# Chunk-selected attention with a gated output stage, rewritten around a list scheduler, shared PSUM banks, quadrant convolution and half-precision bounds

## The chip, the cores and the metric

The kernel runs on one core of one Trainium2 chip. The metric is the device time of one execution in microseconds (us), from the device's own record. The kernel before takes 294.87 us, the median of 3 runs (294.83 to 296.1).

## The reference

Inputs are q, k and v of shape (4 batches, 8 heads, 768 positions, 64 dimensions) in fp32 and three weight arrays. What is computed, cut to what matters:

```python
# attention over the 6 best chunks of 32 keys, per query row
k_chunks = k.reshape(B, H, 24, 32, D)
k_min, k_max = np.min(k_chunks, axis=3), np.max(k_chunks, axis=3)
ub = np.sum(np.maximum(q[..., None, :] * k_min[:, :, None], q[..., None, :] * k_max[:, :, None]), axis=-1)
ub = np.where(causal_chunk, ub, -1e9)
top_chunks = np.argsort(ub, axis=-1)[..., -6:]
scores = (q @ k.T) / 8                       # masked to the chosen chunks and to keys at or before the row
attn = softmax(scores)
x = (attn @ v), heads side by side           # (4, 768, 512)

# gated stage
gate_pre[t, c] = sum over 5 taps i of conv_w[i, c] * x[t - 4 + i, c]   # causal, one filter per channel
out = (sigmoid(gate_pre) * (x @ w_val)) @ w_out                         # w_val, w_out: 512 x 512
```

An upper bound per query and chunk chooses six chunks; attention sees only keys in them; the result goes through a short causal convolution per channel that gates a linear map, and through a second linear map. The output is fp32.

## The kernel before

Two heads make a pair; there are 16 pairs, four to a batch. A pair goes through three lists of steps, and a fourth list holds the gated stage.

- `kq_steps` loads nothing itself (the loads are issued two pairs ahead by `load_kq` and `load_v` on SyncE's queue). It transposes K and Q on TensorE in fp32 with an identity (L155, L178), three 128x128 blocks to a PSUM bank, so each of K and Q takes two halves of 384 columns. ScalarE copies K out, scaled by 1/8, to fp16 (`KE`, L159), and VectorE reduces the same bank to the maximum and minimum of each chunk (L163, L164). `kblock` forms the per-chunk bounds relative to the first chunk (L167 to L172) in fp32 (`KB`). Q is copied to fp32 (`q32`, L181); GpSimd casts it to fp16 (`QU`, L183); VectorE makes max(q, 0) (`rq`, L185). GpSimd casts V to fp16 with a column of ones (`VA`, L190).
- `sel_steps` computes the bounds with fp32 matmuls, max(q,0) times (max - min) plus q times min (L207, L209), for five of the six tiles of 128 rows; the first tile needs no choice. VectorE adds the causal fill (L211), takes the top eight of each row (L219), compares with the sixth (L224) and has TensorE transpose the 0/1 result (L233). The copy of that (L236) goes into spare partitions of `QU`: opposite them in `KE` lie rows with -30 over one chunk each, so the score matmul itself subtracts 30 from the keys of chunks not chosen.
- `attn_steps` computes scores with keys on the partitions and queries on the columns, in banks of 512 columns (L271, L291), takes the exponential on ScalarE into fp16 (L275, L295), zeroes the triangle above the diagonal on GpSimd (L264, L280), multiplies by V with the column of ones for the denominator (L304), divides on VectorE (L306, L307), and transposes the result to channels by positions, `xT` (L314, L316). No maximum is subtracted ahead of the exponential.
- The gated stage works per batch on 128 channels at a time. The convolution is a matmul with diagonal matrices, five taps times a high and a low fp16 part of the weight, so ten matmuls of 384 columns per half (L334). The forty diagonals are built by GpSimd (L379) from `cwT` and `cwl`. ScalarE takes tanh (L339); `moe_val` multiplies by w_val (L348) and VectorE gates it (L352); `moe_out` multiplies by w_out (L359), and ScalarE's copy (L362) is stored (L363).

The order is set by hand. At iteration i the attention of pair i, the selection of pair i+1, the K and Q work of pair i+2 and the gated steps due at i are merged by their relative place in each list:

```python
merge(attn_steps(i), sel_steps(i + 1), kq_steps(i + 2), moe[i])
```

PSUM has three tags: "w" (three banks, every transposition, bound, convolution, value and output), "s" (three banks, scores) and "av" (two banks).

Of the kernel before, what the change touches and what calls it, by code (L numbers as in the profile page):

```python
# [13 lines left out]
AX = mybir.AxisListType  # L14


@with_exitstack
def kernel(
# [10 lines left out]
    nc = tc.nc  # L29
# [8 lines left out]
    PEN = -30.0  # L38
    NPAIR = (B * H) // 2
    HB = S // 2  # L40


    HP = (slice(0, 64), slice(64, 128))
    CP = (slice(64, 64 + NCH), slice(0, NCH))
    KP = (slice(0, 64 + NCH), slice(0, 128))

    CC = (1, 0)
    SELT = NT - 1

    ident_np = np.eye(128, dtype=np.float32)  # L50
    identh_np = np.eye(128, dtype=np.float16)
    e_np = np.zeros((64, S), dtype=np.float16)
    for c in range(NCH):
        e_np[c, c * CH:(c + 1) * CH] = PEN
    cfill_np = np.zeros((128, SELT, 2, NCH), dtype=np.float32)
    for it in range(1, NT):
        for p in range(128):
            cfill_np[p, it - 1, :, (it * 128 + p) // CH + 1:] = -1.0e9
    cfill_np = cfill_np.reshape(128, SELT * 2 * NCH)

    ident_dr = nc.inline_tensor(ident_np, name="identc")
    identh_dr = nc.inline_tensor(identh_np, name="identh")
    e_dr = nc.inline_tensor(e_np, name="echunk")
    cfill_dr = nc.inline_tensor(cfill_np, name="cfill")

    cpool = ctx.enter_context(tc.tile_pool(name="cpool", bufs=1))
    npool = ctx.enter_context(tc.tile_pool(name="npool", bufs=3))
    hpool = ctx.enter_context(tc.tile_pool(name="hpool", bufs=2))
    ppool = ctx.enter_context(tc.tile_pool(name="ppool", bufs=2))
    mpool = ctx.enter_context(tc.tile_pool(name="mpool", bufs=2))  # L70
    ps = ctx.enter_context(tc.tile_pool(name="ps", bufs=3, space=bass.MemoryType.PSUM))

    ident = cpool.tile([128, 128], FP, tag="ident")
    identh = cpool.tile([128, 128], F16, tag="identh")
    cfill = cpool.tile([128, SELT * 2 * NCH], FP, tag="cfill")
    wval_sb = cpool.tile([128, NCT, DM], F16, tag="wval")
    wout_sb = cpool.tile([128, NCT, DM], F16, tag="wout")
    w32 = cpool.tile([128, 2, NCT, DM], FP, tag="w32")
    cwn = cpool.tile([KSZ * NCT, 128], FP, tag="cwn")
    cwT = cpool.tile([128, KSZ * NCT], FP, tag="cwT")  # L80
    cwh = cpool.tile([128, KSZ * NCT], F16, tag="cwh")
    cwl = cpool.tile([128, KSZ * NCT], FP, tag="cwl")
    diag = cpool.tile([128, KSZ * NCT, 2, 128], F16, tag="diag")
    xT = cpool.tile([128, 2 * NCT, S + 4], F16, tag="xT")
    KE = [cpool.tile([128, 2, S], F16, tag=f"KE{i}", name=f"KE{i}") for i in range(3)]
    QU = [cpool.tile([128, 2, S], F16, tag=f"QU{i}", name=f"QU{i}") for i in range(3)]
    VA = [cpool.tile([128, 2, NT, D + 1], F16, tag=f"VA{i}", name=f"VA{i}") for i in range(3)]
    KB = [cpool.tile([128, 2, 2 * NCH], FP, tag=f"KB{i}", name=f"KB{i}") for i in range(2)]
    NS = [cpool.tile([128, SELT, 128], F16, tag=f"NS{i}", name=f"NS{i}") for i in range(2)]

    def bank(shape, dt=FP, tag="w", bufs=3):
        return ps.tile(shape, dt, tag=tag, name=f"ps_{tag}", bufs=bufs)

    nat = {}

    def load_kq(p):
        b, h0 = p // NCT, 2 * (p % NCT)
        kn = npool.tile([128, NT, 128], FP, tag="kn", name="kn")
        qn = npool.tile([128, NT, 128], FP, tag="qn", name="qn")
        vn = npool.tile([128, NT, 128], FP, tag="vn", name="vn")  # L100
        nat[p] = (kn, qn, vn)
        for t, src in ((kn, k), (qn, q)):
            for hh in range(2):
                nc.sync.dma_start(out=t[:, :, hh * 64:(hh + 1) * 64],
                                  in_=src[b, h0 + hh].rearrange("(t p) d -> p t d", p=128))

    def load_v(p):
        b, h0 = p // NCT, 2 * (p % NCT)
        for hh in range(2):
            nc.sync.dma_start(out=nat[p][2][:, :, hh * 64:(hh + 1) * 64],  # L110
                              in_=v[b, h0 + hh].rearrange("(t p) d -> p t d", p=128))


    nc.sync.dma_start(out=ident, in_=ident_dr.ap())
    load_kq(0)
    for i in range(3):
        for hh in range(2):
            nc.sync.dma_start(out=KE[i][HP[1 - hh], hh, :], in_=e_dr.ap())
    nc.sync.dma_start(out=cfill, in_=cfill_dr.ap())
    nc.sync.dma_start(out=identh, in_=identh_dr.ap())  # L120
    load_v(0)
    load_kq(1)
    load_v(1)
    nc.sync.dma_start(out=cwn, in_=moe_conv_w.rearrange("k (c p) -> (k c) p", p=128))
    nc.sync.dma_start(out=w32[:, 0], in_=moe_w_val.rearrange("(ct c) e -> c ct e", c=128))
    nc.sync.dma_start(out=w32[:, 1], in_=moe_w_out.rearrange("(et e) o -> e et o", e=128))

    for i in range(2):
        nc.gpsimd.memset(KB[i], 0.0)
    for i in range(3):  # L130
        nc.vector.memset(QU[i][HP[1], 0, :], 0.0)
        nc.vector.memset(QU[i][HP[0], 1, :], 0.0)
    for i in range(2):
        nc.gpsimd.memset(NS[i], 0.0)
    for i in range(3):
        nc.gpsimd.memset(VA[i][:, :, :, D:D + 1], 1.0)
    nc.vector.memset(xT[:, :, 0:4], 0.0)

    st = {}


    def kq_steps(p):
        kn, qn, vn = nat.pop(p)
        ke, qu, va, kb = KE[p % 3], QU[p % 3], VA[p % 3], KB[p % 2]
        kmx = hpool.tile([128, NCH], FP, tag="kmx", name="kmx")
        kmn = hpool.tile([128, NCH], FP, tag="kmn", name="kmn")
        kmd = hpool.tile([128, NCH], FP, tag="kmd", name="kmd")
        q32 = hpool.tile([128, S], FP, tag="q32", name="q32")
        rq = hpool.tile([128, S], FP, tag="rq", name="rq")
        st[p] = dict(ke=ke, qu=qu, va=va, kb=kb, q32=q32, rq=rq)  # L150

        def khalf(w):
            pt = bank([128, HB])
            for tl in range(3):
                nc.tensor.transpose(out=pt[:, tl * 128:(tl + 1) * 128],  # L155
                                    in_=kn[:, 3 * w + tl, :], identity=ident)
            sl = slice(w * HB, (w + 1) * HB)
            for hh in range(2):
                nc.scalar.activation(out=ke[HP[hh], hh, sl], in_=pt[HP[hh]],  # L159
                                     func=AF.Copy, scale=0.125)  # L160
            cs = slice(w * 12, (w + 1) * 12)
            ptc = pt.rearrange("p (c t) -> p c t", t=CH)
            nc.vector.tensor_reduce(out=kmx[:, cs], in_=ptc, axis=AX.X, op=ALU.max)  # L163
            nc.vector.tensor_reduce(out=kmn[:, cs], in_=ptc, axis=AX.X, op=ALU.min)  # L164

        def kblock():
            nc.vector.tensor_tensor(out=kmd, in0=kmx, in1=kmn, op=ALU.subtract)  # L167
            for hh in range(2):
                hp, c0 = HP[hh], CC[hh] * NCH
                nc.vector.tensor_scalar(out=kb[hp, 0, c0:c0 + NCH], in0=kmd[hp],  # L170
                                        scalar1=kmd[hp, 0:1], scalar2=None, op0=ALU.subtract)
                nc.vector.tensor_scalar(out=kb[hp, 1, c0:c0 + NCH], in0=kmn[hp],  # L172
                                        scalar1=kmn[hp, 0:1], scalar2=None, op0=ALU.subtract)

        def qhalf(w):
            pt = bank([128, HB])
            for tl in range(3):
                nc.tensor.transpose(out=pt[:, tl * 128:(tl + 1) * 128],  # L178
                                    in_=qn[:, 3 * w + tl, :], identity=ident)
            sl = slice(w * HB, (w + 1) * HB)  # L180
            nc.scalar.activation(out=q32[:, sl], in_=pt, func=AF.Copy)  # L181
            for hh in range(2):
                nc.gpsimd.tensor_copy(out=qu[HP[hh], hh, sl], in_=q32[HP[hh], sl])  # L183
            a = max(w * HB, 128)
            nc.vector.tensor_scalar(out=rq[:, a:(w + 1) * HB], in0=q32[:, a:(w + 1) * HB],  # L185
                                    scalar1=0.0, scalar2=None, op0=ALU.max)

        def vcast():
            for hh in range(2):
                nc.gpsimd.tensor_copy(out=va[:, hh, :, 0:D],  # L190
                                      in_=vn[:, :, hh * 64:(hh + 1) * 64])

        return [lambda: khalf(0), lambda: khalf(1), lambda: qhalf(0), kblock, lambda: qhalf(1),
                vcast]
# [254 lines left out]
```

## Time and profile before

| quantity | value |
|---|---|
| median of 3 runs | 294.87 us |
| profiled execution, first to last instruction (span) | 292.5 us |
| runs' median less that span | 2.4 us |
| TensorE matmuls busy | 241.3 us, 82% of the span |
| TensorE weight loads busy (they overlap matmuls) | 171.6 us |
| VectorE, ScalarE, GpSimd busy | 155.2, 160.2, 121.8 us |
| mean granted TensorE clock | 0.959 of full |
| first score matmul in the chain of waits | at 27.07 us |
| DMA moved | 28.46 MB, mean 97 GB/s |

Only the span of the profiled execution is on record, not a separate device time, so the 2.4 us between it and the median of the runs stands for what lies around the span. Busy times of TensorE count every matmul with its passage through the pipeline, and consecutive matmuls overlap; how often a new one starts is read from the chain of waits or from the timeline.

### The profile page before, as it was taken

How to read it: one execution, taken by the hardware profiler on the slowest of the kernel's cores; microseconds unless marked ns; L12 is line 12 of the kernel's file. 1: busy time of each engine (PE TensorE's matmuls, PEld its weight loads, DVE VectorE, ACT ScalarE, POOL GpSimd, SP SyncE). 2: the span in 40 equal slices, each digit the busy share in tenths (PEclk: the TensorE clock that was granted, in tenths of full speed). 3: DMA queues.
4: the chain of work that ended last, by engine and by line, in shares of the span. 5: the costliest groups of instructions: out<-in, count | busy, mean ns of one | idle time of the engine just before them, and what ended most of it. 6: DMA issues, size and time to landing. Idle time of an engine off the chain costs nothing.

```text
span 292.5 us, 5928 instructions
## 1 busy us (share of the span) xinstructions
PE 241.3 (82%) x2161; PEld 171.6 (59%) x2161; DVE 155.2 (53%) x522; ACT 160.2 (55%) x329; POOL 121.8 (42%) x261
## 2 busy tenths in 40 slices
PE   2383926509998897999998999999989999999994
PEld 1181614405757575776666667676757676765551
DVE  3547162404676674858573657666645667631160
ACT  3232713503768659465674774756747765467313
POOL 2416189999254436243433253425251624223000
PEclk9999975956999999999999999999999999999999
DMA  7999992205162554242456343332211000003105
GB/s 165 211 304 245 218 175 54 54 0 110 33 132 55 110 110 99 66 108 56 107 151 159 91 114 86 70 87 61 74 74 38 36 2 0 2 2 143 73 2 215
DMA packets 80746, 28.46 MB, mean 97 GB/s; under 512 B 75962, under 2 KB 76622, under 8 KB 80718
## 3 DMA queue, kind: packets, MB, share of 16 engines
q1 hardware_dynamic: 80718, 28.09, 40.9%
q8 instruction: 17, 0.28, 0.4%
q14 instruction: 11, 0.09, 0.1%
HBM read 21.79 MB, written 6.29 MB: 96 GB/s over the span
## 4 chain that ended last, share of the span: by engine, by line
PE 66%; POOL 12%; ACT 10%; issue 3%; SPq 3%; DVE 2%; DMA 2%; ACTq 0%; POOLq 0%
PE ps_w L334 17%; PE ps_s L271 10%; POOL diag L379 7%; PE ps_av L304 6%; PE ps_w L348 6%; PE ps_w L359 6%; PE ps_w L209 6%; ACT P L275 5%; PE ps_w L207 5%; PE ps_w L155 4%; PE ps_w L178 2%; POOL QU L183 2%; PE ps_w L314 2%; ACT KE L159 2%; ACT osb L362 1%
## 5 line engine op out<-in xcount | busy, mean ns | idle before, releaser
L275 ACT ACTIVATE P<-ps_s 128x512 f16<-128x512 f32 x160 | 87.8, 606 | 57.1 <-PE ps_s L271 56.8
L271 PE MATMUL ps_s<-QU,KE 88*128 88x512 f16 (+5 forms) x224 | 54.9, 336 | 7.1 <-ACT P L275 4.1
L264 POOL TENSOR_SCALAR_AFFINE_SELECT P<-P 128x256 f16<-128x256 f16 (+1 forms) x80 | 29.0, 364 | 71.1 <-ACT P L275 58.3
L334 PE MATMUL ps_w<-xT,diag 128*128 128x384 f16 x320 | 57.8, 331 | 0.0
L304 PE MATMUL ps_av<-VA,P 128*128 128x65 f16 x672 | 33.4, 196 | 21.9 <-POOL P L264 19.9
L304 PEld LDWEIGHTS <-P 128*128 128x128 f16 x672 | 28.4, 99 | 32.0 <-POOL P L264 26.2
L159 ACT ACTIVATE KE<-ps_w 64x384 f16<-64x384 f32 x64 | 31.0, 485 | 26.9 <-PE ps_w L155 26.5
L183 POOL CAST QU<-q 64x384 f16<-64x384 f32 x64 | 35.1, 548 | 24.6 <-ACT q L181 22.7
L334 PEld LDWEIGHTS <-diag 128*128 128x128 f16 x320 | 31.0, 99 | 21.4 <-issue 1.9
L339 ACT ACTIVATE g<-ps_w 128x384 f32<-128x384 f32 x32 | 15.9, 498 | 30.5 <-PE ps_w L334 30.5
L209 PE MATMUL ps_w<-KB,q 128*128 128x48 f32 x160 | 32.3, 285 | 0.0
L163 DVE TENSOR_REDUCE kmx<-ps_w 128x12 f32<-128x384 f32 x32 | 17.8, 555 | 26.7 <-ACT KE L159 26.6
L236 DVE COPY QU<-ps_w 24x640 f16<-24x640 f16 x32 | 15.5, 484 | 29.9 <-PE ps_w L233 29.4
L207 PE MATMUL ps_w<-KB,rq 128*128 128x48 f32 x160 | 31.2, 278 | 0.0
L271 PEld LDWEIGHTS <-KE 88*128 88x128 f16 (+1 forms) x224 | 21.1, 101 | 16.8 <-issue 10.8
L280 POOL TENSOR_SCALAR_AFFINE_SELECT P<-P 128x256 f16<-128x256 f16 x32 | 13.1, 408 | 31.4 <-ACT P L275 31.3
L207 PEld LDWEIGHTS ps_w<-KB,rq 128*128 128x128 f32 x160 | 25.9, 202 | 0.3
L155 PE MATMUL ps_w<-ident,kn 128*128 128x128 f32 x96 | 17.7, 300 | 9.7 <-DMA kn<-in_k_dram 9.7
L209 PEld LDWEIGHTS ps_w<-KB,q 128*128 128x128 f32 x160 | 25.7, 202 | 0.0
L348 PE MATMUL ps_w<-xT,wval_sb 128*128 128x384 f16 x128 | 23.9, 325 | 1.8 <-ACT q L181 1.8
L190 POOL CAST VA<-vn 128x384 f16<-128x384 f32 x32 | 16.5, 516 | 20.4 <-PE ps_av L304 12.9
L359 PE MATMUL ps_w<-wout_sb,gv 128*128 128x512 f16 x96 | 23.8, 379 | 0.7 <-ACT osb L362 0.7
(46 smaller groups left out, 309.0 us busy)
## 6 DMA issues: line engine op xcount, KB each, us to landing
kn<-in_k_dram SPq DMA_DIRECT2D x32, 192.0 KB, 3.3
qn<-in_q_dram SPq DMA_DIRECT2D x32, 192.0 KB, 3.4
vn<-in_v_dram SPq DMA_DIRECT2D x32, 192.0 KB, 3.3
out_dram<-osb SPq DMA_DIRECT2D x24, 256.0 KB, 2.0
w<-in_moe_w_val_dram SPq DMA_DIRECT2D x1, 1024.0 KB, 5.6
w<-in_moe_w_out_dram SPq DMA_DIRECT2D x1, 1024.0 KB, 7.9
KE<-echunk SPq DMA_DIRECT2D x6, 96.0 KB, 2.7
cfill<-cfill SPq DMA_DIRECT2D x1, 120.0 KB, 2.3
```

The lines of the kernel that those rows point to most:

```text
L155: nc.tensor.transpose(out=pt[:, tl * 128:(tl + 1) * 128], in_=kn[:, 3 * w + tl, :], identity=ident)
L159: nc.scalar.activation(out=ke[HP[hh], hh, sl], in_=pt[HP[hh]], func=AF.Copy, scale=0.125)
L183: nc.gpsimd.tensor_copy(out=qu[HP[hh], hh, sl], in_=q32[HP[hh], sl])
L207: nc.tensor.matmul(out=pu[:, it - 1, :], lhsT=rq[:, ts], rhs=kb[:, 0, :], start=True, stop=False)
L209: nc.tensor.matmul(out=pu[:, it - 1, :], lhsT=q32[:, ts], rhs=kb[:, 1, :], start=False, stop=True)
L264: nc.gpsimd.affine_select(out=ap, in_=ap, pattern=[[0, n], [1, 128]], compare_op=ALU.is_ge, fill=0.0, base=0, channel_multiplier=-1)
L271: nc.tensor.matmul(out=pq[:, col:col + n], lhsT=ke[KP[hh], hh, jt * 128:(jt + 1) * 128], rhs=qu[KP[hh], hh, q0:q0 + n], start=True, stop=True)
L275: nc.scalar.activation(out=pt, in_=pq, func=AF.Exp)
L304: nc.tensor.matmul(out=pav[:, qt, :], lhsT=where[hh, jt, qt], rhs=va[:, hh, jt, :], start=(jt == 0), stop=(jt == qt))
L334: nc.tensor.matmul(out=pg, lhsT=diag[:, ki * NCT + ct, part, :], rhs=xT[:, slot, w * HB + ki:w * HB + ki + HB], start=(n == 0), stop=(n == ...
L348: nc.tensor.matmul(out=pv, lhsT=wval_sb[:, ct, et * 128:(et + 1) * 128], rhs=xT[:, slot0 + ct, 4 + w * HB:4 + (w + 1) * HB], start=(ct == ...
L359: nc.tensor.matmul(out=po, lhsT=gv[b, et][:, s * 128:(s + 1) * 128], rhs=wout_sb[:, et, :], start=(et == 0), stop=(et == NCT - 1))
```

## The change

The kernel is written again with the same stages. The parts:

1. **Order.** Every step is a `Node` with an engine, a guessed duration, its reads and writes and a priority. `Plan.schedule` is a list scheduler that places the nodes on the engines' queues and issues the program in the order of the starts it finds. Offsets of each kind of step from its pair's base (`OFF`, in ns, with `PERIOD` between pairs) are constants.
2. **PSUM.** One tile holds all eight banks. A step asks for one bank or an aligned two, and the scheduler hands them out. So K and Q are transposed into two banks and copied in one instruction of 768 columns, both heads' scores go into two banks and one exponential of 1024 columns, and both heads' AV results are divided in one instruction.
3. **Bounds.** q is split into fp16 high and low parts (`QH`, `QL`), max(q,0) likewise (`RH`, `RL`), and the chunk bounds likewise (`KB`). Six fp16 matmuls of 48 columns per tile replace the two fp32 ones; the first tile takes two. `KB` is no longer relative to the first chunk, and only the four chunks on the diagonal get the causal fill.
4. **Softmax guard.** The largest bound of a row becomes a 33rd row beside the 24 mask rows (copied by `m`), opposite a row of -0.125, and the exponential adds 10: the exponent is score - bound/8 + 10.
5. **Convolution.** Once per batch and two 128-channel slots, all work is in 64x64 diagonals. For each tap and part, four matmuls go to the four quarters of the array: rows 0-63 or 64-127 of a slot (`r`) and slot `c` of the two. The 64x64 diagonals are built by two VectorE multiplies instead of forty GpSimd ones. The columns of w_val and rows of w_out are loaded in the matching channel order.
6. **Engines.** K is scaled to fp16 by GpSimd from an SBUF copy, K's reductions read that copy, Q's casts are VectorE's, one half of the mask copy is ScalarE's. Constants (identities, mask rows, fill) are made on the chip by GpSimd and no longer loaded. Loads go into four buffers; output has four buffers, and the last batch's evictions alternate between ScalarE and VectorE. Eight matmuls on zeros open TensorE's queue.

The core of the diff (a line of dots marks what is left out):

```diff
-    merge(kq_steps(0))
-    merge(sel_steps(0), kq_steps(1))
-    for i in range(NPAIR):
...
+    def schedule(self):
...
+                t0 = min(c[0] for c in cand)
+                t, n, pick = min((c for c in cand if c[0] <= t0 + self.slack),
+                                 key=lambda c: (c[1].prio, c[1].i))
...
+    order = plan.schedule()
+    with tc.manual_schedule():
+        for n in order:
+            n.fn()

-    ps = ctx.enter_context(tc.tile_pool(name="ps", bufs=3, space=bass.MemoryType.PSUM))
+    psum = pp.tile([128, 8, 512], FP, tag="psum", name="psum")

-                nc.tensor.matmul(out=pu[:, it - 1, :], lhsT=rq[:, ts], rhs=kb[:, 0, :],
-                                 start=True, stop=False)
-                nc.tensor.matmul(out=pu[:, it - 1, :], lhsT=q32[:, ts], rhs=kb[:, 1, :],
-                                 start=False, stop=True)
+            for it in range(1, NT):
+                n = 0
+                for lhs, part, kind in ((QH, 0, 1), (RH, 0, 0), (QH, 1, 1), (RH, 1, 0), (QL, 0, 1), (RL, 0, 0)):
+                    term(it, lhs, kbs(part, kind), n == 0, n == 5)
+                    n += 1

+        add(f"K32{p}", ACT, t_act(S), 124, base + OFF["KT"], lambda: nc.scalar.activation(
+            out=K32[w].rearrange("p (a n) -> p a n", a=2), in_=b3(kbk)[:, :, 0:HB], func=AF.Copy),
+            [("kps", p)], [("K32", w)], [kbk])
+                lambda h=h: nc.gpsimd.tensor_scalar(out=KE[t3][HP[h], h, :], in0=K32[w][HP[h]],
+                                                    scalar1=0.125, scalar2=None, op0=ALU.mult),
+            lambda: nc.vector.tensor_copy(out=QH[w], in_=Q32[w]), [("Q32", w)], [("QH", w)])
+            lambda: nc.vector.tensor_scalar(out=RH[w], in0=QH[w], scalar1=0.0, scalar2=None, op0=ALU.max),
+                lambda h=h: nc.vector.tensor_copy(out=QU[t3][HP[h], h, :], in_=QH[w][HP[h]]),
+            lambda: nc.gpsimd.tensor_tensor(out=QL[w][:, 128:S], in0=Q32[w][:, 128:S],
+                                            in1=QH[w][:, 128:S], op=ALU.subtract),
+            lambda: nc.vector.scalar_tensor_tensor(out=RL[w][:, 128:S], in0=QH[w][:, 128:S], scalar=0.0,
+                                                   in1=QL[w][:, 128:S], op0=ALU.is_gt, op1=ALU.mult),

-            nc.scalar.activation(out=pt, in_=pq, func=AF.Exp)
+                out=pt[:, :, 0:n], in_=psum[:, bk.at:bk.at + 2, 0:n], func=AF.Exp, bias=bias),

-            for ki in range(KSZ):
-                for part in range(2):
-                    nc.tensor.matmul(out=pg, lhsT=diag[:, ki * NCT + ct, part, :],
-                                     rhs=xT[:, slot, w * HB + ki:w * HB + ki + HB],
-                                     start=(n == 0), stop=(n == 2 * KSZ - 1))
+                    for n in range(2 * KSZ):
+                        ki, part = n // 2, n % 2
+                        for r in range(2):
+                            rp = HP[r]
+                            for c in range(2):
+                                nc.tensor.matmul(out=psum[HP[c], gb.at + r, 0:HB],
+                                                 lhsT=diag[rp, part, ki * NCT + 2 * j + c, :],
+                                                 rhs=xT[rp, s0 + 2 * j + c, hw * HB + ki:hw * HB + ki + HB],
+                                                 start=(n == 0), stop=(n == 2 * KSZ - 1))

-                nc.gpsimd.tensor_scalar(out=diag[:, i, part, :], in0=identh,
-                                        scalar1=w[:, i:i + 1], scalar2=None, op0=ALU.mult)
+                nc.vector.tensor_tensor(
+                    out=diag[:, part], in0=i64.unsqueeze(1).to_broadcast([128, n, 64]),
+                    in1=src.unsqueeze(2).to_broadcast([128, n, 64]), op=ALU.mult)
+            eng = DVE if last and s % 2 else ACT
```

## The prediction

> **What bounds the kernel now.** I read the page first: TensorE (PE) is busy 82% of 292.5 us, no other engine over 55%. Stretch by stretch (busy us of each engine, granted clock, DMA share, GB/s) this is not one regime:
>
> ```profile
> 20.00:50.00 30.00, 15.67 (x113) 10.64 (x112) 14.56 (x51) 10.84 (x24) 18.60 (x33) 0.83 0.99 188
> 50.00:100.00 50.00, 37.59 (x360) 27.30 (x359) 24.85 (x88) 26.91 (x57) 34.22 (x68) 0.86 0.34 74
> 150.00:200.00 50.00, 47.14 (x452) 33.85 (x451) 31.90 (x113) 33.19 (x70) 21.04 (x47) 1.00 0.43 107
> ```
>
> The columns after the length are PE, weight loads, VectorE (DVE), ScalarE (ACT), GpSimd (POOL). From 100 us on PE is the bound, with 47 of 50 us; before that POOL is busier than later, PE is half idle and its clock is down to 0.83 of full. The chain of waits (start, length, engine, what, count) says why, and gives the steady period:
>
> ```profile
> 24.43 1.97 DVE rq L185
> ...
> 38.73 6.37 POOL diag L379 x10
> ...
> 137.00 0.41 PE ps_av L304 x13
> ...
> 138.69 3.26 PE ps_w L334 x20
> ...
> 144.98 0.86 PE ps_w L359 x4
> ...
> 192.20 1.31 PE ps_w L348 x8
> ...
> 198.63 3.26 PE ps_w L334 x20
> ...
> 285.97 0.61 ACT osb L362
> 286.59 2.02 DMA out_dram<-osb
> ```
>
> Building the forty diagonals (L379, 24.9 us of POOL) holds the early pairs. Then the convolution of every fourth pair stands 59.94 us apart (138.69 to 198.63), so a pair costs 14.98 us.
>
> **What a pair costs PE.** A group's mean ns counts the pipeline's depth; what queues is the step from one start to the next, and the chain shows it: convolution 3.26/20 = 0.163 us for 384 columns, value 1.31/8 = 0.163, output 0.86/4 = 0.216 for 512 (so 0.00042 per column), attention times V 0.41/13 = 0.032. The timeline shows the two fp32 kinds:
>
> ```profile
> 206.00 0.39 PE L207 MATMUL ps_w<-KB,rq 128*128 128x48 f32 x2
> 206.22 0.39 PE L209 MATMUL ps_w<-KB,q 128*128 128x48 f32 x2
> ...
> 207.78 0.51 PE L155 MATMUL ps_w<-ident,kn 128*128 128x128 f32 x3
> 208.13 0.38 PE L271 MATMUL ps_s<-QU,KE 88*128 88x512 f16 x1
> ```
>
> Two fp32 bound records per 0.22, so 20 per pair are 2.20; three fp32 transposes take 0.35 or less (0.11 each). A pair now: transposes 12 x 0.11 = 1.3, bounds 2.2, mask transposes 5 x 0.055 = 0.3, scores 5376 columns = 2.26, AV 42 x 0.032 = 1.34, back transposes 0.33, convolution 20 x 0.163 = 3.26, value 1.3, output 6 x 0.216 = 1.3. Sum 13.6; the other 1.4 of the 14.98 is PE waiting. Over 16 pairs PE has 217 us of work, so 75 of the span are start, waits and tail.
>
> **The change, part by part.**
> *Bounds in fp16.* Twenty fp32 records go (2.20). Thirty-two fp16 matmuls of 48 columns come, each like an AV matmul (65 columns, own weights, 0.032): 1.02. Gain 1.18 per pair.
> *Convolution in quadrants.* Per batch four groups of ten steps, each step four 64x64 matmuls of 384 columns in four different quarters of the array. No row shows quarters. If the four run beside each other a step is one stream, 0.163, and a group 1.63; if they queue, four streams, 0.652 and 6.52. Issue doesn't forbid the first: AV shows a load and a matmul every 0.032, so forty pairs issue in 1.28. I take 1.63, the row of the same 384 columns, because each of the four uses its own partitions in, its own partitions or bank out, and nothing in the order stands between them. Per pair (a group per pair) 1.63 instead of 3.26.
> The Trainium skill, "TensorEngine Tiling (Array Packing)", Tiling Modes, says that tiles load and multiply in parallel, which agrees with 1.63. The same page speaks against it under Restrictions: column tiling switches off the fast weight load; "TensorE: Matmul & The Clock Gate", LDWEIGHTS, prices a load at columns/1.2 ns, so four loads of 64 would be about 0.213 per step, and as an estimate the total would grow by 8 us. No row here shows it.
> *The rest of PE.* A sixth mask transpose (0.33 for six), and weights with 97 rows instead of 88, free (88 and 128 rows both stream 512 columns in the same step). A pair after: 1.3 + 1.02 + 0.33 + 2.26 + 1.34 + 0.33 + 1.63 + 1.3 + 1.3 = 10.8; sixteen, 173 us.
> *ACT.* L275 starts every 0.48 for 512 columns, L295 0.27 for 256: 0.06 + 0.00083 per column. After, per pair: K and Q copies and one mask half, each 768 wide (3 x 0.69), five exponentials of 1024 and one of 256 (5 x 0.90 + 0.27), tanh 0.69, 1.5 outputs (0.72): 8.25. The guard is a bias and one more weight row, so nothing here. Covered by 10.8.
> *DVE.* L163 repeats every 0.47 for 384, so about 1.04 ns per column plus 0.06. Per pair: two reductions of 768 (1.72), normalising (0.87), gating (0.87), two PSUM copies of 768 at L316's rate (0.95), eleven top-8 steps (0.82), comparison, fill, reciprocal (0.54), key bounds (0.55), QH (0.46), RH and two QU copies (0.26 each, if narrow copies run at twice the fp32 rate; 0.46 each if not), RL 0.73: about 8.3 to 8.9.
> *POOL.* The diagonals' 24.9 go to DVE as two multiplies of 1280 columns (2.8). L264 takes 0.41 for 256 and 0.29 for 128; casts 0.51 for 384 and 1.9 to 2.07 for 2048. Per pair: four triangles (2.1), V cast (0.85), two KE scalings of 768 (0.85 each as casts; L379's 0.60 for 128 columns is the high end, 3.6), QL with two inputs (between a cast, 0.74, and 3.0 at L379's rate; I double the cast, 1.5), guard copy 0.15: 6.3. The low values are nearer, being plain streams like the casts; at the high ends POOL would hold 13.3 per pair, 16 x 13.3 + 24 of start, tail and surroundings = 237.
> *A price hidden in that.* The row that speaks against it, from the timelines of POOL and DVE:
>
> ```profile
> 24.12 2.07 POOL L366 CAST wval_sb<-w 128x2048 f16<-128x2048 f32 x1
> ...
> 24.36 2.04 DVE L185 TENSOR_SCALAR rq<-q 128x384 f32<-128x384 f32 x1
> ```
>
> An SBUF-to-SBUF DVE step that takes 0.36 at 215.00 in the same timeline lasted 2.04 here, as long as POOL's cast beside it ran. The new DVE work has five such steps per pair (QH, RH, QU twice, RL) and some small ones. The mean of the 16 wide L185 rows is 0.590, so 0.23 over 0.36; nine such waits are 2.1, DVE 10.4 to 11.0 per pair. That is beside a pair of 12.2 (below), so I charge nothing, with up to 12.2 - 11 of cover left.
> The Trainium skill, "SBUF — State Buffer", section on two separate sides, states this as an exclusive lock for a whole instruction; by that rule each of the nine can lose a full POOL instruction, and the estimate would be that of the whole of rival 3.
> *Start.* First scores stand at 27.07 now. After: the keys are the first load; POOL builds constants until about 8.3 (0.8 in, 0.8 of identities, 5.7 of mask rows: a memset like L134's 0.63 for 640, four selects of 768 at 0.87, two memsets; 1.0 of fills), scales KE to 10.0, makes QL to 11.5, DVE makes RL to 12.2, bounds, top-8 and comparison to 14.3, transposes and copies to 15.3; eight hand-overs of 0.16 to 0.2 (a matmul lasts 0.33 while the next starts at 0.163): 17. By then PE has done 4.0 of its 173.
> *Waits and tail.* The list order and the shared banks move everything, and no row prices that. Ends: no waits at all, or twice now's. I keep the 1.4 per pair, since the stages and their lengths are the same: 23. After PE's last matmul 6.6 pass now (285.9 to 292.5); with a fourth output buffer the last eviction no longer waits: 4.5.
> *Sum.* 17 + 169 + 23 + 4.5 = 213.5 of span. The median of the runs, 294.87, is 2.4 over the profiled span of 292.5, so 216.
>
> **The rivals.**
> 1. Forecast: quarters beside each other, PE still the bound. 216, by itself 204 (waits halved) to 228 (waits half as long again). Chance 0.62.
> 2. Quarters overlap only in twos, or their loads queue: a step is 0.326 or something between. Up to 16 x 1.63 = 26 more: 225 to 242. For: no row shows four at once. Against: 0.032 per load and matmul. 0.16.
> 3. The order doesn't hold: DVE loses a whole POOL instruction (6.3 / 9 = 0.7 on average) at each of nine steps, so DVE is 8.3 + 6.3 = 14.6 per pair and the bound. 16 x 14.6 + 17 + 4.5 + 2.4 = 258, halfway 237. For: 24.36. Against: most L185 rows wait far less. 0.12.
> 4. The other side: the convolution doesn't do what it says; quarters queue and their loads are not covered, each matmul costing its stream and a load of 0.099 (the mean of LDWEIGHTS on L334), 0.262. 640 x 0.262 = 168 instead of 26: 358. It decides from 0.164 per quarter matmul on: there 640 x 0.164 = 105 instead of 26 eats the whole gain of 79. With covered loads, 0.163, it comes to 294, no change: 0.04. Slower: 0.06.
>
> **How the numbers follow.** Faster is rivals 1 to 3, 0.90; same 0.04; slower 0.06. About 0.5% is what a measurement of this kernel can tell from no change. The range takes the forecast's own ends and reaches through rival 2 and the halfway case of 3: 204 to 245.
>
> **What would show it.** Convolution steps of about 0.163 for four records (right), 0.33 or 0.65 (rivals 2, 4); the bound matmuls 0.032 apart; first scores near 17 us; no POOL diagonals; a pair's period near 12.2 with PE over 85% busy between 60 and 190 us and full clock. Wrong: PE idle ended mostly by DVE or POOL, DVE steps on SBUF data several times their shortest, KE scalings of 3 us.

## The result, and the profile after

The changed kernel takes 261.4 us (median of 4 runs, 259.9 to 262.8) beside 294.9 before: a ratio of 0.886, with a 95% interval of 0.881 to 0.891. The direction was right; the size was not. 216 was forecast, 261.4 lies outside 204 to 245, and the gain is 33 us where 79 were expected.

The stretches of the changed kernel (length, then busy us of PE, weight loads, DVE, ACT and POOL, granted clock, DMA share, GB/s):

```profile
0.00:20.00 20.00, 7.72 (x33) 4.31 (x33) 15.34 (x25) 3.72 (x4) 17.36 (x28) 0.74 1.01 228
20.00:50.00 30.00, 22.40 (x254) 17.18 (x255) 25.48 (x79) 16.84 (x19) 21.15 (x20) 0.72 0.86 208
50.00:100.00 50.00, 36.86 (x572) 26.47 (x572) 41.17 (x122) 33.71 (x40) 41.10 (x46) 0.97 0.51 113
100.00:150.00 50.00, 40.85 (x552) 29.14 (x549) 46.98 (x122) 34.13 (x43) 33.96 (x32) 0.97 0.41 101
150.00:200.00 50.00, 41.29 (x632) 28.85 (x633) 39.36 (x106) 31.62 (x39) 33.09 (x34) 0.97 0.15 44
200.00:250.00 50.00, 46.09 (x641) 29.72 (x640) 20.06 (x52) 28.91 (x37) 13.19 (x20) 1.00 0.13 49
```

Before, PE was busy 47 of 50 us from 100 us on. Now it is busy 37 to 41 through the middle and gets back to 46 only after 200 us, when the last keys have been prepared. From 50 to 100 us DVE and POOL are the fullest engines, at 41 each; then DVE alone, at 47; from 150 to 200 no engine is over 42. The steps wait for one another across engines, as the chain of waits shows further down. The costliest groups show what lies on POOL (busy us, mean ns of one, then the idle time before it):

```profile
L440 POOL TENSOR_SCALAR KE<-K 64x768 f16<-64x768 f32 x32 | 72.3, 2258 | 23.1 <-PE psum L577 19.2
L598 POOL TENSOR_SCALAR_AFFINE_SELECT P<-P 128x512 f16<-128x512 f16 (+1 forms) x64 | 36.1, 580 | 27.0 <-ACT P L584 26.2
L655 PE MATMUL psum<-xT,diag 64*64 64x384 f16 x640 | 28.7, 329 | 2.2 <-DVE xT L634 2.2
L459 POOL TENSOR_TENSOR QL<-Q,QH 128x640 f16<-128x640 f32 x16 | 22.9, 1432 | 9.8 <-DVE QH L450 8.5
```

One scaling of K to KE takes 2.26 us on average, 2.12 at its shortest, where the forecast took 0.85. The chain of waits goes over three engines in nearly equal parts, and by line it names KE first; between 121 and 129 us (start, length) four POOL steps stand in it one behind the other:

```profile
PE 32%; DVE 27%; POOL 26%; issue 7%; ACT 6%; POOLq 0%; ACTq 0%; DVEq 0%
POOL KE L440 15%; PE psum L674 6%; PE psum L655 6%; PE psum L577 5%; PE psum L695 5%; POOL QL L459 4%; DVE QU L456 3%; ACT P L584 3%; PE psum L607 3%; PE psum L481 3%; DVE KK L421 3%; POOL P L598 3%; PE psum L411 2%; DVE RL L463 2%; DVE KB
...
121.23 2.13 POOL KE L440
123.43 2.18 POOL KE L440
125.67 1.96 POOL P L598 x3
127.64 1.47 POOL QL L459
```

The chain before was this:

```profile
PE 66%; POOL 12%; ACT 10%; issue 3%; SPq 3%; DVE 2%; DMA 2%; ACTq 0%; POOLq 0%
```

The start is late as well; the first scores stand at 28.04 in the changed kernel's chain:

```profile
6.80 0.74 POOL etile L297
7.94 0.89 DVE KE L303
...
14.42 1.37 DVE KB L431
...
18.92 1.35 DVE RL L463
20.32 1.18 PE psum L481 x25
...
28.04 1.86 PE psum L577 x8
```

PE's own terms came out as forecast. In PE's timeline two convolution groups (80 quadrant matmuls) run through without a break:

```profile
212.13 3.46 PE L655 MATMUL psum<-xT,diag 64*64 64x384 f16 x80
215.52 0.51 PE L535 MATMUL psum<-identh,NS 128*128 128x128 f16 x6
```

From 212.13 to 215.52 are 3.39 us for twenty steps, 0.17 each; within a step the four quarters start within some 0.01 us of one another, and the next four mostly 0.163 after them.

### The profile page after: what moved, and what is told of

Its sections match the earlier page's. It is cut to its first block, busy times and chain, and to the rows that moved or that the text cites. A ratio compares the mean times of both kernels' runs of the same rounds, so it can differ in the third digit from the quotient of the medians.

```text
span 258.2 us, 6734 instructions
## 1 busy us (share of the span) xinstructions
PE 199.6 (77%) x2697; PEld 137.5 (53%) x2697; DVE 190.5 (74%) x503; ACT 150.7 (58%) x182; POOL 159.8 (62%) x178
## 4 chain that ended last, share of the span: by engine, by line
PE 32%; DVE 27%; POOL 26%; issue 7%; ACT 6%; POOLq 0%; ACTq 0%; DVEq 0%
POOL KE L440 15%; PE psum L674 6%; PE psum L655 6%; PE psum L577 5%; PE psum L695 5%; POOL QL L459 4%; DVE QU L456 3%; ACT P L584 3%; PE psum L607 3%; PE psum L481 3%; DVE KK L421 3%; POOL P L598 3%; PE psum L411 2%; DVE RL L463 2%; DVE KB L431 2%
## 5 line engine op out<-in xcount | busy, mean ns | idle before, releaser
L584 ACT ACTIVATE P<-psum,bias 128x1024 f16<-128x1024 f32 x96 | 92.2, 1006 | 14.4 <-PE psum L577 14.4
L440 POOL TENSOR_SCALAR KE<-K 64x768 f16<-64x768 f32 x32 | 72.3, 2258 | 23.1 <-PE psum L577 19.2
L577 PE MATMUL psum<-QU,KE 97*128 97x512 f16 (+7 forms) x256 | 51.9, 317 | 8.2 <-ACT QU L545 3.1
L598 POOL TENSOR_SCALAR_AFFINE_SELECT P<-P 128x512 f16<-128x512 f16 (+1 forms) x64 | 36.1, 580 | 27.0 <-ACT P L584 26.2
L577 PEld LDWEIGHTS <-KE 97*128 97x128 f16 (+1 forms) x256 | 22.5, 100 | 19.2 <-issue 12.5
L655 PE MATMUL psum<-xT,diag 64*64 64x384 f16 x640 | 28.7, 329 | 2.2 <-DVE xT L634 2.2
L607 PE MATMUL psum<-VA,P 128*128 128x65 f16 x672 | 25.8, 195 | 5.4 <-POOL P L598 4.0
L421 DVE TENSOR_REDUCE KK<-K 128x24 f32<-128x768 f32 x32 | 29.3, 940 | 0.1
L459 POOL TENSOR_TENSOR QL<-Q,QH 128x640 f16<-128x640 f32 x16 | 22.9, 1432 | 9.8 <-DVE QH L450 8.5
L695 PE MATMUL psum<-wout,GV 128*128 128x512 f16 x96 | 24.7, 389 | 5.4 <-DVE xT L634 2.4
L663 ACT ACTIVATE G<-psum 128x768 f32<-128x768 f32 x16 | 13.0, 812 | 19.9 <-PE psum L655 19.9
L674 PE MATMUL psum<-xT,wval 128*128 128x384 f16 x128 | 23.7, 336 | 0.2 <-ACT K L416 0.2
L547 DVE COPY QU<-psum 33x768 f16<-33x768 f16 x16 | 9.0, 561 | 18.3 <-ACT QU L545 10.4
```

Of the source, the lines that this page charges most:

```text
L421: lambda i=i, op=op: nc.vector.tensor_reduce(out=KK[w][:, i, :], in_=K32[w].rearrange("p (c t) -> p c t", t=CH), axis=AX.X, op=op), [("K32 ...
L440: lambda h=h: nc.gpsimd.tensor_scalar(out=KE[t3][HP[h], h, :], in0=K32[w][HP[h]], scalar1=0.125, scalar2=None, op0=ALU.mult),
L459: lambda: nc.gpsimd.tensor_tensor(out=QL[w][:, 128:S], in0=Q32[w][:, 128:S], in1=QH[w][:, 128:S], op=ALU.subtract),
L577: nc.tensor.matmul(out=psum[:, bk.at + h, col:col + m], lhsT=KE[t3][KP[h], h, jt * 128:jt * 128 + 128], rhs=QU[t3][KP[h], h, q0:q0 + m], s ...
L584: add(f"e{nm}_{p}", ACT, t_act(2 * n), 124, pr, lambda pt=pt, bk=bk, n=n: nc.scalar.activation(out=pt[:, :, 0:n], in_=psum[:, bk.at:bk.at ...
L598: nc.gpsimd.affine_select(out=ap, in_=ap, pattern=pat, compare_op=ALU.is_ge, fill=0.0, base=0, channel_multiplier=-1)
```

## The experiments

Theory A: the price of the KE scaling, 2.26 us instead of 0.85, fills POOL and through it DVE. Theory B: the order that the scheduler planned, and not what a step costs, leaves PE waiting. Theory C: POOL blocks DVE whatever the length of POOL's steps.

**Casts in place of the scaling.**

```diff
-  nc.gpsimd.tensor_scalar(out=KE..., in0=K32..., scalar1=0.125, scalar2=None, op0=ALU.mult)
+  nc.gpsimd.tensor_copy(out=KE..., in_=K32...)
-  PEN = -40.0                  # and -0.125 in the guard row
+  PEN = -320.0                 # and -1.0 in the guard row
-  func=AF.Exp, bias=bias)
+  func=AF.Exp, bias=bias, scale=0.125)
```

> The two KE steps of a pair become plain GpSimd casts without the factor 1/8, which goes into the exponential's scale (mask row -320, guard row -1); the planned order is the same instruction for instruction. Theory A (the price of the KE scaling, 2.26 us each where 0.85 was assumed, is what fills GpSimd and, through it, VectorE): KE 0.83 to 0.95 us, GpSimd 6.6 us per pair, SBUF-to-SBUF VectorE steps nearer their shortest, time 225 to 238. Theory B (the order itself, not a price, leaves TensorE waiting): time 252 or more. Theory C (any GpSimd work blocks VectorE, whatever its length): VectorE's QU and RH steps stay at a mean of 0.52 and 0.91 and the time at 245 or more.

239.5 us (239.0 to 239.6), 22 less than the changed kernel, with the same order. POOL's cast of the same 64 x 768, and the stretches:

```profile
L440 POOL CAST KE<-K 64x768 f16<-64x768 f32 x32 | 28.1, 877 | 21.4 <-PE psum L576 17.1 <-ACT K L416 3.3
```

```profile
50.00:100.00 50.00, 40.29 (x634) 29.03 (x633) 47.86 (x124) 35.01 (x42) 36.45 (x51) 1.00 0.58 127
100.00:150.00 50.00, 44.25 (x670) 31.76 (x669) 46.91 (x140) 38.95 (x48) 28.48 (x41) 1.00 0.33 88
```

The cast costs 0.88, as the forecast had assumed for the scaling. B is out as the main cause, since the order is the same; A is right, though 239.5 is just above its range. What is left shows in the third busy column: DVE, at 47 to 48 of 50, has become the fullest. Its steps on SBUF data hardly shortened (RH 0.91 to 0.86 us, QU 0.52 to 0.46), which was one of C's signs; C's time, 245 or more, did not come.

**KE on ScalarE.** The two scalings of a pair move, from the same SBUF copy; the scheduler places them anew.

```diff
-  add(f"ke{h}_{p}", POOL, t_pool(S), 100, ...  nc.gpsimd.tensor_scalar(out=KE..., in0=K32..., scalar1=0.125, ...
+  add(f"ke{h}_{p}", ACT, t_act(S), 124, ...  nc.scalar.activation(out=KE..., in_=K32..., func=AF.Copy, scale=0.125)
```

> The two KE scalings of a pair move from GpSimd to ScalarE (64 x 768 from the SBUF copy); the planner places them anew. Theory A: GpSimd falls to 4.9 us per pair, VectorE's SBUF steps come nearer their shortest than with the casts, ScalarE rises by 1.6 to about 11.7 busy (10 queued) per pair, still under the pair's 12: 225 to 240, like the casts. Theory B: 252 or more. Theory C: clearly below the casts, 218 to 225, since GpSimd then meets VectorE least.

239.4 us (239.1 to 239.7): the same as the casts. POOL is busy only 28.8 and 20.5 us of the two stretches, and still nothing more is won, so C's 218 to 225 is out. ACT, at 41.6 and 44.1 of 50, took what POOL gave up.

**A nearer price in the planner only.** At 2.25 us, about the measured mean, the list scheduler finds no order; the price tried is 1.95.

```diff
-  add(f"ke{h}_{p}", POOL, t_pool(S), 100, ...
+  add(f"ke{h}_{p}", POOL, 1950.0, 100, ...
```

> Only the planner's price of a KE step changes, 1.95 us where it was 0.88, so the order is made for steps nearly as long as they are; the instructions are the changed kernel's own. Theory B (the order was wrong for the true length): time falls to 235 to 248. Theory A (the work itself, and what it blocks on VectorE): within 5 us of 261.

254.8 us (253.9 to 255.7), 6.5 less: between the two. An order made for nearly the true length gets back some 6 us; with casts in the old order 22 come back. The order is a part, the smaller one.

**Quarter by quarter.** The loops over the quarters go outside the loop over the ten taps and parts.

```diff
-  for n in range(2 * KSZ):
-      for r in range(2):
-          for c in range(2):
+  for r in range(2):
+      for c in range(2):
+          for n in range(2 * KSZ):
```

> The forty matmuls of a convolution group are issued quarter by quarter (ten taps and parts in a row in one quarter of the array) and not in turn. If the overlap comes from neighbours in the queue standing in different quarters: a group takes about 6.5 us where it took 1.5 to 1.6, 16 x 4.9 = 78 more of TensorE, and the time rises to 310 to 335. If the engine finds work for the other quarters in its queue by itself: a group stays near 1.6 to 2 and the time at 261. In between: 3.3 per group, about 285.

291.8 us (three runs from 291.3 to 292.1, one at 301.2), 30 more than the changed kernel, and within 1.6% of the kernel before. Two groups in the chain:

```profile
252.10 8.80 PE psum L655 x80
```

A group takes 4.2 us from its first start to its last instead of 1.5 (4.4 instead of 1.7 in the chain): neither the 6.5 of no overlap nor 1.6. The order of the quarters in the queue makes the overlap, though not all of it. Of the 43 us of PE work that it adds, 30 reach the end; the rest fills PE's waits.

**Constant rows loaded.** The mask and guard rows of KE come from six loads behind the first pair's instead of GpSimd and six VectorE copies.

```diff
-  add("etile", POOL, 4 * t_pool(S) + 800, 100, -8e5, mk_e, (), ["etile"])
+  e_dr = nc.inline_tensor(e_np, name="echunk")
-  add(f"ke_e{i}{h}", DVE, ...  nc.vector.tensor_copy(out=KE[i][HP[1 - h], h, :], in_=etile[HP[1 - h], :])
+  add(f"ke_e{i}{h}", SP, ...  nc.sync.dma_start(out=KE[i][HP[1 - h], h, :], in_=e_dr.ap())
```

> The mask and guard rows of KE are loaded (six loads of 96 KB behind the first pair's) and no longer made by GpSimd (5.1 us) and copied by VectorE (six steps, 0.35 to 0.93 each); all else as in the changed kernel. If the late start (first scores at 28.0 us, 17 forecast) comes from these constants: first scores at 19 to 22 and 5 to 9 us off the whole, 252 to 256. If it comes from VectorE's chain behind them: first scores at 25 or later and the time within 3 us of 261.

256.3 us (three runs from 256.2 to 256.9, one at 252.6). First scores at 19.9 instead of 28.0, but only some 5 us at the end by the medians, with runs that lie 4 us apart.

**GpSimd narrow.** From pair 3 on, GpSimd's steps for KE, QL, VA and the triangles touch a few columns, in the same places, with the same waits. The rest keeps old values, so only the time means something.

```diff
-  nc.gpsimd.tensor_scalar(out=KE[t3][HP[h], h, :], in0=K32[w][HP[h]], ...
+  nc.gpsimd.tensor_scalar(out=KE[t3][HP[h], h, 0:8], in0=K32[w][HP[h], 0:8], ...
-  nc.gpsimd.tensor_tensor(out=QL[w][:, 128:S], ...
+  nc.gpsimd.tensor_tensor(out=QL[w][:, 128:136], ...
-  nc.gpsimd.tensor_copy(out=VA[t3][:, :, :, 0:D], ...
+  nc.gpsimd.tensor_copy(out=VA[t3][:, :, :, 0:1], ...
-  ap = pt[:, :, 0:128]          # the triangle
+  ap = pt[:, :, 0:4]
```

> From pair 3 on GpSimd's steps keep their places and waits and touch 4 to 12 columns instead of 256 to 768 (so K, V, the low parts of q and the triangles are left at old values); the order is the changed kernel's. It shows what is left when GpSimd neither takes time nor blocks. Theory A and C (GpSimd's time and its blocking are the loss): VectorE's QU steps at 0.34 to 0.36 and RH at 0.30, time 220 to 228. If VectorE's own work or the order is the loss: 235 or more with VectorE still over 90% busy between 50 and 150 us.

228.4 us (227.9 to 228.7), 33 less than the changed kernel and 11 less than the casts. The stretches:

```profile
50.00:100.00 50.00, 44.80 (x689) 33.69 (x690) 45.70 (x147) 37.31 (x45) 20.28 (x54) 0.97 0.64 143
100.00:150.00 50.00, 47.59 (x706) 34.53 (x706) 42.04 (x132) 42.12 (x52) 8.18 (x39) 1.00 0.37 96
```

PE is the bound again from 100 us on, at 47.6 of 50, as forecast. RH's mean falls from 0.91 to 0.48, QU's from 0.52 to 0.42; from the fifth pair on they are 0.34 and 0.36, against shortest steps of 0.30 and 0.34. So what GpSimd costs here, by its length, its lateness and its blocking together, is 33 of the 45 us that the forecast was short.

**The QU copies on ScalarE**, on top of the casts.

```diff
-  add(f"qu{h}_{p}", DVE, ...  nc.vector.tensor_copy(out=QU[t3][HP[h], h, :], in_=QH[w][HP[h]])
+  add(f"qu{h}_{p}", ACT, ...  nc.scalar.activation(out=QU[t3][HP[h], h, :], in_=QH[w][HP[h]], func=AF.Copy)
```

> The KE casts of the first experiment (239.5), and besides the two QU copies of a pair on ScalarE instead of VectorE. There VectorE was 95% busy between 50 and 150 us. If VectorE, with its waits for GpSimd, bounds that stretch: VectorE loses 0.9 to 1.0 us per pair, the time falls by 6 to 12 to 228 to 234. If TensorE or the order bounds it: 237 to 241.

243.3 us (240.8 to 243.4), slower than the casts alone by up to 4: the second expectation missed too, on the upper side. DVE's load fell to 45.9 and 40.4 of 50, but ACT needs 0.84 for a copy that DVE does in 0.36 when free, and ACT rose to 42.2 and 45.6.

**Casts and loaded constants.** The two diffs above together, with -320 and -1 in the loaded rows.

> KE by plain casts and its constant rows loaded: the first experiment (239.5) and the one with the loaded constants (256.3) together. If the late start is a loss of its own, it shows whole once GpSimd no longer fills the middle: first scores at 19 to 21 and 229 to 233. If VectorE's bound stretch swallows an earlier start, as with the slow KE: 235 to 240.

237.0 us (236.2 to 238.2). First scores at 18.8, 8 us earlier than with casts alone, and 2.5 us at the end. DVE is why:

```profile
20.00:50.00 30.00, 21.07 (x243) 14.65 (x242) 28.30 (x79) 21.05 (x24) 19.89 (x26) 0.91 1.05 241
50.00:100.00 50.00, 40.59 (x642) 30.91 (x640) 48.11 (x134) 33.24 (x39) 32.65 (x46) 0.97 0.64 140
```

It is 95% busy from 20 us to 150 (46.85 of 50 in the last third). The early start goes into that queue.

**Prices of the exponential and VectorE's waits in the planner**, on top of that: these prices alone:

```diff
-  add(f"kb{p}", DVE, 550, ...
+  add(f"kb{p}", DVE, 1060, ...
-  add(f"rh{p}", DVE, t_dve(S, 0.27), ...
+  add(f"rh{p}", DVE, t_dve(S, 0.27) + 530, ...
-  add(f"qu{h}_{p}", DVE, t_dve(S, 0.27), ...
+  add(f"qu{h}_{p}", DVE, t_dve(S, 0.27) + 120, ...
-  add(f"e{nm}_{p}", ACT, t_act(2 * n), ...
+  add(f"e{nm}_{p}", ACT, (97.0 + 0.878 * 2 * n), ...
```

QH and RL get 0.05 and 0.1 more.

> The kernel with casts and loaded constants; only the planner's prices change, to what the traces show: exponential 1.0 us, and VectorE's steps on SBUF data with their mean waits. If the order still loses to wrong prices: 3 to 8 us under that kernel. If the queues' content is the limit: within 2 us of it, either way.

235.0 us (234.3 to 235.8), 2 less; the intervals of the two ratios, 0.793 to 0.802 and 0.800 to 0.811, overlap. At most a small gain.

**RH on ScalarE**, on casts and loaded constants.

```diff
-  add(f"rh{p}", DVE, ...  nc.vector.tensor_scalar(out=RH[w], in0=QH[w], scalar1=0.0, scalar2=None, op0=ALU.max)
+  add(f"rh{p}", ACT, ...  nc.scalar.activation(out=RH[w], in_=QH[w], func=AF.Relu)
```

> The kernel with casts and loaded constants, and RH = max(QH, 0) made by ScalarE (Relu) and not by VectorE, where it takes a mean of 0.86 us with waits and 0.30 without. ScalarE gets 0.85 per pair. If VectorE is the bound in the middle and ScalarE has room: 3 to 8 us under that kernel. If ScalarE's queue takes over, as with the two QU copies (243 instead of 239.5): 0 to 5 us over it.

232.9 us (232.2 to 233.3), 4 less. One step that takes 0.85 of DVE is worth 0.84 of ACT; the two QU copies, tried above on the casts alone, cost ACT 1.68 for 0.93 of DVE and were not.

**Bounds back in fp32**, on casts and loaded constants: `Q32` and max(Q32, 0) times fp32 bounds, QH, QL, RH and RL gone.

```diff
-  KB = [sb([128, 2, 2, 2, NCH], F16, ...
+  KB = [sb([128, 2, 2, NCH], FP, ...
-  for lhs, part, kind in ((QH, 0, 1), (RH, 0, 0), (QH, 1, 1), (RH, 1, 0), (QL, 0, 1), (RL, 0, 0)):
-      term(it, lhs, kbs(part, kind), n == 0, n == 5)
+  term(it, Q32, kbs(1), True, False)
+  term(it, RQ, kbs(0), False, True)
-  add(f"ub{p}", PE, 32 * 31.5, ...
+  add(f"ub{p}", PE, 12 * 220.0, ...
```

> The kernel with casts and loaded constants, with the bounds undone to fp32: twelve fp32 matmuls (24 records of 0.11 us) per pair for thirty-two of 0.025, so TensorE gets 1.8 us more per pair; QH, QL, RH and RL go, max(q, 0) stays in fp32, QU is cast from the fp32 copy. VectorE loses about 2 us per pair with its waits, GpSimd the 1.4 of QL. If VectorE and GpSimd are the bound in the middle: the fp16 bounds cost more than they give, and this is faster by 4 to 12. If TensorE is near its bound: slower by 5 to 25.

259.9 us (257.5 to 260.8), 23 more. A group of bounds takes 2.5 us from its first start to its last instead of 0.78, and these matmuls make up 17% of the chain of waits. The fp16 split is worth it, even though it loads DVE and GpSimd.

**Narrow GpSimd and loaded constants.**

The two diffs above together, the scaling of KE kept.

> From pair 3 on GpSimd's steps touch a few columns only, as in the earlier narrow kernel (228.4), which leaves K, V, the low parts of q and the triangles at old values, and the constant rows of KE are loaded. If the late start is the rest of the difference to the forecast of 216: first scores at 19 to 20 and 217 to 222. If VectorE's own work swallows the earlier start, as it did with the casts (237.0 instead of 239.5): 225 to 228.

222.3 us (222.0 to 222.6), 6 less than narrow alone, and just above the range; first scores at 19.9. The late start is half of the remaining 12.

**Work on a scratch tile that nobody waits for.** In the narrow kernel, two `tensor_scalar` of 64 x 128 on scratch after each triangle.

```diff
+  for i in range(2):
+      nc.gpsimd.tensor_scalar(out=SCO[i], in0=SCI, scalar1=0.125, scalar2=None, op0=ALU.mult)
```

> The narrow kernel (228.4; the same parts left at old values), and after each of the four narrow triangle steps of a pair GpSimd does two scalings of 64 x 128 on a scratch tile that nobody reads or waits for: eight of 0.6 us, 4.8 us of GpSimd per pair, while its useful steps are delayed by no more than about 1.2 us each and have idle time before them. If GpSimd's activity alone blocks VectorE's SBUF steps: QU (mean 0.42 there) to 0.5 or more, RH (0.48) to 0.65 or more, and 232 to 240. If only waiting for GpSimd's results cost time: VectorE's steps as in the narrow kernel and 228 to 231.

231.5 us (231.0 to 231.6) beside 228.4: 3 more, between the two expectations. RH's mean rises from 0.48 to 0.53 and QU's from 0.42 to 0.46. POOL is as busy again as with the casts (29.9 of 50 us between 100 and 150, 28.5 there), and the time is 8 us shorter. So work that nobody waits for does lengthen DVE's steps, but in pieces of about 0.5 us it costs at most 3 us, the delay of GpSimd's useful steps behind it included. What shares the rest of the 33, the length of its real steps, their late results or blocking by pieces of 2 us, was not tried apart.

**All that helped, and the casts of the key bounds on ScalarE.**

Casts, loaded constants, prices and RH on ScalarE, and:

```diff
-  nc.vector.tensor_copy(out=KB[w][hp, 0, :, 1 - h, :], in_=KK[w][hp])
+  nc.scalar.activation(out=KB[w][hp, 0, :, 1 - h, :], in_=KK[w][hp], func=AF.Copy)
```

> Casts, loaded constants and RH on ScalarE (232.9), with the planner's prices of the exponential and of VectorE's SBUF steps set to the traces' (2 us less where tried alone), and the two small high-part casts of the key bounds on ScalarE instead of VectorE (0.78 us per pair there with waits, two steps of about 0.25 on ScalarE). If VectorE is still what ends last: 226 to 231. If ScalarE, busy 41 of 50 us already, takes over: 232 to 237.

231.9 us (231.5 to 232.8), between the two expectations; ratio 0.788 (0.784 to 0.791), not to be told from RH on ScalarE alone (0.786 to 0.795). Both beat the kernel before and the changed one; ACT is at 45 of 50 between 100 and 150 us.

## Why the prediction was wrong

*The term that failed first: two KE scalings at 0.85.* The prediction saw a POOL scaling in the trace (L379, 0.60 for 128 columns), named its rate as the high end, 3.6 us, and took the cast's because both are plain streams. It measured 2.26, about as far from the one as from the other. But L379's row pointed the right way: 2.13 at the median for 768 columns and 0.60 for 128 make 2.4 ns per column and 0.3 fixed, against 0.82 to 0.88 us for a cast of 768. Taking only a fixed part off it would have come closer: 0.17 by the two sizes of cast in the forecast leaves, as an estimate, 2.8 for 768 columns. Casts in its place: 22 of the missing 45 us.

*The cover that failed with it: "I charge nothing".* The prediction counted 2.1 of DVE's waits behind GpSimd per pair and called them covered. Their size was about right. From the changed kernel's trace, sorted by whether a GpSimd instruction was under way when the step began (mean us):

| DVE step | GpSimd idle | GpSimd under way |
|---|---|---|
| QU from QH (SBUF) | 0.35 (10 of 32) | 0.60 (22) |
| KB casts (SBUF) | 0.18 (23 of 32) | 0.57 (9) |
| RL, two SBUF inputs | 0.82 (3 of 16) | 0.96 (13) |
| mask half from PSUM (L547) | 0.56 (7 of 16) | 0.56 (9) |
| chunk reductions of an SBUF copy (L421) | 0.95 (7 of 32) | 0.94 (25) |

Copies, casts and two-input steps on SBUF wait; copies from PSUM and reductions don't. RH, at 0.95 with GpSimd under way (15 of 16) against its shortest 0.30, is hit hardest. The excess over the idle times, RH's over its shortest, adds up to 1.8 us per pair over all copies, casts and two-input steps on SBUF. The Trainium skill, "SBUF — State Buffer", section on two separate sides, calls it an exclusive lock for whole instructions, which these rows fit. What failed is the cover. DVE is busy 125.9 of the 150 us between 40 and 190, so it is held up without being full: each step of a pair waits for the one before across POOL, DVE and PE, whose shares of the chain are 26, 27 and 32%, and the loss is the length of that chain, not a sum on one engine. With POOL narrow, 33 of the 45 us are gone; how they divide between DVE's blocking and GpSimd's late results no run separates.

*Waits of PE at 1.4 per pair, "since the stages and their lengths are the same".* Between the last AV matmuls of pairs 0 and 10 lie 139.6 us in the changed kernel, 14.0 per pair, against 12.2 forecast; with the casts 124.7, 12.5; in the narrow kernel with loaded constants 116.9, 11.7. So the term nearly holds once KE costs what the forecast took, and is undershot once GpSimd is out of the way.

*The start at 17.* It was 28.0. The POOL part up to 8.3 was right (its constants end at 8.6). The six VectorE copies of the mask rows stand in no term; on SBUF data beside POOL they take until 11.9, and only then begin the reductions, QH and the key bounds. The first of the bounds' casts, 0.18 without GpSimd, lasts 1.37, as long as GpSimd's QL runs beside it (the DVE line holds two casts):

```profile
14.27 1.49 POOL L459 TENSOR_TENSOR QL<-Q,QH 128x640 f16<-128x640 f32 x1 [1.25 <-DVE KK L424]
14.42 2.15 DVE L431 CAST KB<-KK 64x48 f16<-64x48 f32 x2
```

Loading the rows brings 18.8 to 19.9. It is worth 6 us where PE is the bound, 2.5 where DVE is. The granted clock between 20 and 50 us is 0.72, below the 0.83 before; what that costs the start no run separates.

*The tail at 4.5, from 6.6.* The 6.6 was misread: before, PE's last matmul ends at 288.5 and not at 285.9, so 4.0 us pass after it; 3.7 pass now. The term was nearly right, but not for its reason.

*Right:* the quarters side by side (0.163 per step, no row had shown it), transposes, scores, AV; fp16 bounds even cheaper than assumed (0.78 per 32, 0.025 each, not 0.032); PE over 85% busy between 60 and 190 us at full clock, but only once GpSimd has less to do (80% at 0.96 in the changed kernel, 88% at 1.00 with the casts, 95% in the narrow kernel with loaded constants). The prediction's own third rival came nearest: DVE held up at GpSimd, 237 to 258; only the full DVE that it assumed is not there.

*The sum again:* 261.4, less 22 for the KE price, less 11 for the rest of GpSimd, less 6 for the start, is 222.3. Of the remaining 6 to 216, some 3 are the start, 19.9 instead of 17. The rest lies between the first scores and PE's last matmul, 196.6 us where 169 + 23 were forecast, and its cause stays open; DVE is still at 47.8 of 50 between 50 and 100 us in that kernel:

```profile
50.00:100.00 50.00, 44.49 (x709) 33.59 (x708) 47.79 (x156) 39.47 (x48) 17.38 (x53) 1.00 0.68 149
100.00:150.00 50.00, 48.04 (x712) 34.85 (x711) 42.34 (x132) 40.62 (x52) 8.65 (x41) 1.00 0.30 80
```

## What to carry to other kernels

Price a new instruction by a row of the same operation on the same engine, with a fixed part taken off for the difference in size, before a row of the same shape; where the two are far apart, the low one alone does not belong in the forecast. When work moves off the bounding engine onto two others that hold each other up, their busy shares are no cover: neither needs to be full for the bound to move there. An early start is worth its full time only if the engine that is next in line has room to take it.

## What the runs showed of the hardware

GpSimd's scaling by a constant of 64 x 768 from fp32 to fp16 takes 2.13 us at the median (2.12 at the shortest), its cast of the same data 0.82; a scaling of 64 x 8 takes 0.23.

Four 64x64 matmuls in four quarters of the array start within some 0.01 us and a step of four takes 0.163 us, as long as one 128x128 matmul of 384 columns; issued quarter by quarter, forty take 4.2 us from first start to last instead of 1.5. A load of 64x64 weights takes 0.106, no less than the 0.099 of 128x128. The Trainium skill, "TensorEngine Tiling (Array Packing)", Restrictions, says that column tiling loses the fast load; the durations fit that, but the estimate of 0.213 per step did not come: the four loads of a step start within some 0.01 us as well, and run beside the matmuls.

A matmul of 48 columns with its own weights follows the one before after 0.025 us at full clock.
